# First MLP product of a block in two passes of half its tokens, two chunks of F per PSUM bank

## The chip, the core and the metric

The kernel runs on one core of a Trainium2 chip. Its engines are TensorE (PE in the profile, with PEld for its weight loads), VectorE (DVE), ScalarE (ACT), GpSimd (POOL) and SyncE (SP, which issues DMAs); each works through its own queue in order and waits on semaphores for the others. The metric is the device time of one execution in microseconds; the number compared is the median of several runs.

## What is computed

A block of 2048 tokens of width 640: a layernorm, sliding-window attention of 32 heads of 20 with a window of 256, and beside it an MLP of width 1536 with a squared ReLU, whose output gates the attention's.

```python
xn = _layernorm(x, axis=-1)
s = _A_ref(xn, A_wqkv, A_wo)                     # 32 heads, window 256, output times wo
g = _silu(_B_ref(xn, B_w1, B_b1, B_w2, B_b2))    # relu(xn @ w1 + b1)**2 @ w2 + b2
return x + s * g
```

Every large matrix is carried as a high and a low part in float32r, and a product is made of three: high by high, high by low, low by high.

## The kernel before

**Stages.** A first stage normalizes and transposes the tokens and makes v and the first part of q and k. Then the attention runs in 268 steps of one pair of heads and one tile of 128 tokens each: scores (L493), their transposed form (L542), exponentials on ACT (L549), masks on POOL, splits into float16 parts on ACT and DVE, and the product with v (ops, L481). Last comes the product with wo (L654).

**The filler.** Between the parts of each attention step the function `fill` takes work from one generator, `filler`: the rest of q and k (qkps), then the MLP, in eight blocks. A block is one half of F (768 = 6 chunks of 128, NFH = 6) and one quarter of the tokens (BT = 512). It has a first product (hps: w1 by xn, then bias, ReLU and square) and a second (yps: the squares by w2). Each `yield` names what the piece costs in the plan; `fill` takes pieces until the step's share is reached, and a `yield None` ends the step's filling early.

**Two halves of the array.** The filler's matmuls contract over 128 rows as two matmuls of 64 rows, one on the upper half of TensorE's rows (front, index 0) and one on the lower (back, index 1), which run beside each other. Both add into the same PSUM bank, and a back may not start while the group's fronts still write there. So the fronts of one group are emitted among the backs of the group before. `halves` emits a front through `ahead` and puts the back into the group's `Job`; `ahead` emits backs as long as the plan's clock of the lower half lies behind that of the upper; `open_for` lets a job's backs go only once its `after` is set, which happens with its last front. When its last back is out, `done` queues the evacuation, which `soon` and `flush` emit a little later.

**Banks.** All filler groups share three PSUM banks (`Acc`, tags mm0 to mm2). A group can be opened when one of them has been given back in the program's order (`free`, in the evacuation); if none has, the waiting evacuations are emitted at once. On the chip the group's first matmul then waits until the last reader of that bank is done.

**First product, before.** For each of the six chunks of F one group fills a bank with 128 features of all 512 tokens: 15 matmuls of 512 columns per half. Its evacuation works on two halves of the tokens (MT = 256 columns): ReLU and square on ACT (L951, L952), the exact square on DVE (sq, L954), the low part on POOL (hl, L955). The first half is emitted with `evac`, the second (`rest`, through `late`) a little later, and frees the bank. `hs` holds the chunks whose first half is made, `whole` those that are complete.

**Second product, before.** For each of the block's four tiles of 128 tokens (tt) and each half of the 640 outputs (nh) one group sums 18 matmuls of 320 columns per half over the six chunks; DVE adds the bias or the other half of F's part (ysb, L984) and frees the bank. `product` waits in the program's order until its chunk is in `hs` (tt < 2) or `whole`. For tt = 0 the two groups (nh = 0 and 1) are opened one after the other with the first four chunks each, and then both are ended with the last two (L1008 to L1015).

Of the kernel before, what the change touches and what calls it, by code (L numbers as in the profile page):

```python
# [9 lines left out]
F32 = mybir.dt.float32  # L10
F32R = mybir.dt.float32r
BF16 = mybir.dt.bfloat16
F16 = mybir.dt.float16
AF = mybir.ActivationFunctionType
ALU = mybir.AluOpType

P = 128
S = 2048
D = 640
# [4 lines left out]
KC = D // P  # L24
NP = H // 2
NB = 4
BT = S // NB
# [4 lines left out]
HALF = D // 2  # L32
NFH = F // 2 // P
FHALF = F // 2
MT = 256
# [8 lines left out]
COST = {61: 0.0285, P: 0.067, 2 * P: 0.12, HALF: 0.147, 3 * P: 0.172, BT: 0.23}  # L44
# [9 lines left out]
def f32(ap):  # L54
    return ap.bitcast(F32)
# [3 lines left out]
def attn_mlp_kernel(ctx: ExitStack, tc, x, wqkv, wo, w1, b1, w2, b2, out):  # L59
    nc = tc.nc  # L60
# [47 lines left out]
    b1t = const.tile([P, F // P], F32, name="b1t")  # L108
# [8 lines left out]
    wgt = ctx.enter_context(tc.tile_pool(name="wgt", bufs=2))  # L117
# [19 lines left out]
    with tc.tile_pool(name="ph1v", bufs=2) as p1v, tc.tile_pool(name="ph1", bufs=2) as p1, tc.tile_pool(name="ph1x", bufs=4) as p1b, tc.tile_pool(name="ph1w", bufs=1) as p1w:  # L137
# [137 lines left out]
        with tc.manual_schedule(engines={E_.PE, E_.Activation, E_.DVE, E_.Pool, E_.SP}):  # L275
# [90 lines left out]
            for w in "kq":  # L366
                ps = pat.tile([P, BT // 2], F32, tag="s", name="qkps")
# [111 lines left out]
    def half(j, out, a, b_, **kw):  # L479
        r = slice(j * HP, (j + 1) * HP)  # L480
        return nc.tensor.matmul(out, a[r], b_[r], skip_group_check=True, **kw)  # L481
# [188 lines left out]
        def free(self):  # L670
            banks.append(self.bank)

    def halves(job, ps, a, b_, first, last):
        cost = COST[ps.n]

        def front():
            job.mark = half(0, ps.tile, a, b_, start=first, stop=False)

        def back():
            if first:  # L680
                wait_for(job.mark)
            half(1, ps.tile, a, b_, start=False, stop=last)
        ahead(front, cost)
        job.items.append((back, cost))
        if last:
            job.after = clock[0]

    def open_job(evac, *then):
        def done():
            pending.append(evac)  # L690
            ended.append((mark(), clock[1]))
            for f in then:
                f()
        job = Job(done)
        backlog.append(job)
        return job

    def mm_halves(ps, mms, work, evac, *then):
        job = open_job(evac, *then)
        for j, (a, b_) in enumerate(mms):  # L700
            halves(job, ps, a, b_, j == 0, j == len(mms) - 1)
            yield work
# [9 lines left out]
    def lin1(tiles, off, n):  # L712
        t, o = divmod(off, KC * BT)
        return tiles[t][:, o:o + n]
# [157 lines left out]
    def filler():  # L872
# [5 lines left out]
        for g, b in order_qk:  # L878
# [9 lines left out]
            for w in "qk":  # L888
# [3 lines left out]
                def evac(ps=ps, w=w, g=g, b=b):  # L892
                    vload[0] += 0.7
                    hi = stg.tile([P, BT], F32R, tag="stg", name="shm")
                    lo = stg.tile([P, BT], F32R, tag="stg", name="slo")
                    split(hi, lo, ps.tile)
                    ps.free()
                    posts.extend(qk_stores(w, slice(g * P, (g + 1) * P), slice(b * BT, (b + 1) * BT), hi, lo))
# [19 lines left out]
        for n, (hf, b) in enumerate(blocks):  # L918
            if n % NB == 0:
                ensure(f"1{hf}")  # L920
            if n == NB - 1:
                w1t[1] = queue_w1(1)
                w2t[1] = queue_w2(1)
                shut.update(("11", "21"))
            if n == last:
                wo_part = queue_wo()
                shut.add("o")
            ensure_bulk(its)
            wt1 = w1t[hf]()
            hs, whole, nxt = {}, set(), []  # L930

            def used(n=n, b=b, nxt=nxt):
                if n == NB - 1:
                    shut.discard("11")
                if n == last:
                    shut.discard("o")
                if n < last and blocks[n + 1][1] != b:
                    nxt.extend(load_xb(blocks[n + 1][1]))
            for fc in range(NFH):
                ps = Acc(BT, "hps")  # L940

                def evac(ps=ps, fc=fc, fi=hf * NFH + fc, hs=hs, whole=whole):
                    hh = [stg.tile([P, BT], F32R, tag="stg", name="hh"),
                          stg.tile([P, BT], F32R, tag="stg", name="hl") if fc < NFH - 4 else wgt.tile([P, D], F32R, tag=f"wg{'kq'[fc % 2]}l", name="hl")[:, :BT]]
                    hs[fc] = hh

                    def part(h):
                        vload[0] += 0.5
                        sl = slice(h * MT, (h + 1) * MT)
                        r = at2.tile([P, MT], F32, tag="relu", name="relu")  # L950
                        nc.scalar.activation(r, ps.tile[:, sl], AF.Relu, bias=b1t[:, fi:fi + 1])  # L951
                        nc.scalar.activation(hh[0][:, sl], r, AF.Square)  # L952
                        sq = at2.tile([P, MT], F32, tag="sq", name="sq")
                        nc.vector.scalar_tensor_tensor(sq, ps.tile[:, sl], b1t[:, fi:fi + 1], r, ALU.add, ALU.mult)  # L954
                        nc.gpsimd.tensor_sub(hh[1][:, sl], sq, f32(hh[0][:, sl]))  # L955
                    part(0)

                    def rest():
                        part(1)
                        whole.add(fc)  # L960
                        ps.free()
                    late.append(rest)
                yield from mm_halves(ps, [(lin1(wt1, (wp * KC + c) * FHALF + fc * P, P), xb[xp][:, c * BT:(c + 1) * BT]) for c in range(KC) for wp, xp in ((0, 0), (0, 1), (1, 0))], 0.213, evac, *([used] if fc == NFH - 1 else []))
            if n % NB == 0:
                ensure(f"2{hf}")
            if n == NB:
                load_yin(0)
                load_yin(1)
            wt2 = w2t[hf]()
            for tt in range(4):  # L970
                t = b * 4 + tt
                place = [None]
                jobs = []

                def start(nh, hf=hf, t=t, place=place, idx=4 * (n - NB) + tt, end=n == NB - 1 and tt == 3, n=n, tt=tt):
                    sl = slice(nh * HALF, (nh + 1) * HALF)
                    ps = Acc(HALF, "yps")

                    def evac():
                        vload[0] += 0.5  # L980
                        if not nh:
                            place[0] = wgt.tile([P, D], F32, tag="wgqh", name="ysb")
                        ysb = place[0]
                        nc.vector.tensor_add(ysb[:, sl], ps.tile, (yins[t] if hf else b2t)[:, sl])  # L984
                        ps.free()
                        if nh:
                            post(y_d[hf][:, t, :], ysb)
                            if hf:
                                del yins[t]
                                load_yin(idx + 2)  # L990
                            if end:
                                shut.discard("21")
                    return [ps, open_job(evac), 0]

                def product(jb, nh, fc):
                    ps, job, _ = jb
                    while fc not in (hs if tt < 2 else whole):
                        if pending or late:
                            flush()
                            yield None  # L1000
                        else:
                            drain(backlog, 1)
                    for hp, wp in ((0, 0), (0, 1), (1, 0)):
                        jb[2] += 1
                        halves(job, ps, hs[fc][hp][:, tt * P:(tt + 1) * P], lin1(wt2, (wp * NFH + fc) * D + nh * HALF, HALF), jb[2] == 1, jb[2] == 3 * NFH)
                        yield 0.133
                jbs = {}
                if tt == 0:  # L1008
                    for nh in range(2):
                        jbs[nh] = start(nh)  # L1010
                        for fc in range(NFH - 2):
                            yield from product(jbs[nh], nh, fc)
                    for nh in range(2):
                        for fc in range(NFH - 2, NFH):
                            yield from product(jbs[nh], nh, fc)  # L1015
                else:
                    for nh in range(2):
                        jbs[nh] = start(nh)
                        for fc in range(NFH):
                            yield from product(jbs[nh], nh, fc)  # L1020
                if n == last and tt % 2:
                    load(0)
                    load(1)
            if n < last and nxt:
                xb, its = nxt
            else:
                its = []
# [214 lines left out]
```

## Time and profile before

| | us |
|---|---|
| median of three runs | 1058.17 |
| lowest and highest | 1046.88, 1058.91 |
| the profiled execution | 1057.88 |
| its span, first to last instruction | 1056.2 |

In the profile a line "engine line waited for" tells which instruction an engine stood still before, and which instruction's end released it. The filler's matmuls all stand at L481, so they are told apart by the tile that they write: qkps, hps, yps, and ops for the attention's own. The granted clock is the share of TensorE's clock pulses that its throttle let through. The busy time of PE counts an instruction until its end, so matmuls that run one behind the other overlap in it.

### The profile page before, as it was taken

To read this page: it belongs to the slowest core of one execution; us is meant where nothing else is said; L and a number is where in the kernel's file an instruction comes from. 1 tells how busy PE (TensorE), PEld (TensorE's weight loads), DVE (VectorE), ACT (ScalarE), POOL (GpSimd) and SP (SyncE) were. 2 spreads that over 40 slices of the span, in tenths; PEclk is the share of its full clock that TensorE was granted. 3 is DMA by queue.
4 is the path that set the end of the run, shared out by engine and by line. 5 is a ranking of instruction groups with operands and counts; after the bars stand their busy time and mean duration, and the time that the engine had idled before them with its cause. 6 is when DMAs were issued, how large, how long until landed. Compare 5 with 4: busy or idle time off the path is not lost. (4 is left out here: it accounts for less than half of the span.)

```text
span 1056.2 us, 32767 instructions
## 1 busy us (share of the span) xinstructions
PE 940.2 (89%) x12928; PEld 863.9 (82%) x12928; DVE 754.8 (71%) x2085; ACT 652.1 (62%) x1240; POOL 501.9 (48%) x800
## 2 busy tenths in 40 slices
PE   9999999999998798896897779789889788989998
PEld 9999989988877787786786677678778677878998
DVE  7763689989997686686687678678668756834554
ACT  5533377877887586576477558657747755863221
POOL 5100035755577475566366546557646645652000
PEclk9999999999999998998899899899799889989999
DMA  7996777877853334331542233544254253107674
GB/s 255 344 389 231 218 255 230 252 252 216 257 158 129 107 91 145 90 90 46 170 135 51 83 105 96 155 130 115 65 167 125 56 179 96 34 22 241 247 259 145
DMA packets 106097, 169.77 MB, mean 161 GB/s; under 512 B 42072, under 2 KB 59608, under 8 KB 103384
## 3 DMA queue, kind: packets, MB, share of 16 engines
q1 hardware_dynamic: 105944, 167.68, 50.3%
q8 instruction: 102, 1.67, 0.7%
q14 instruction: 51, 0.42, 0.1%
HBM read 96.15 MB, written 70.91 MB: 158 GB/s over the span
## 5 line engine op out<-in xcount | busy, mean ns | idle before, releaser
L549 ACT ACTIVATE p<-stps,ebias 128x384 f32<-128x384 f32 (+2 forms) x512 | 258.7, 558 | 220.1 <-PE stps L542 126.2
L481 PE MATMUL yps<-w,hh 64*128 64x320 f32 x1536 | 292.0, 340 | 76.1 <-DVE ysb L984 37.5
L503 DVE CUSTOM_DVE_ANT_0 junk<-sps,mask 128x384 bf16<-128x384 f32 (+2 forms) x512 | 250.8, 526 | 129.1 <-PE sps L493 88.6
L550 POOL TENSOR_SCALAR_AFFINE_SELECT p<-p 128x256 f32<-128x256 f32 x256 | 157.8, 616 | 323.1 <-ACT p L549 227.9
L481 PEld LDWEIGHTS yps<-w,hh 64*128 64x128 f32 x1536 | 220.4, 201 | 92.7 <-DVE ysb L984 47.0
L481 PE MATMUL hps<-xb,w 64*128 64x512 f32 x1260 | 256.8, 418 | 21.3 <-DVE ysb L984 10.7
L563 DVE TENSOR_TENSOR pl<-p,ph 128x768 f16<-128x768 f32 (+2 forms) x256 | 243.4, 951 | 16.0 <-PE ops L481 14.0
L481 PE MATMUL ops<-vp,ph 64*128 64x61 bf16 x2880 | 215.1, 193 | 0.1
L481 PE MATMUL yps<-w,hl 64*128 64x320 f32 x768 | 208.1, 333 | 5.8 <-POOL hl L955 5.8
L481 PE MATMUL ops<-vp,pl 64*128 64x61 bf16 x2880 | 212.2, 192 | 0.0
L557 ACT ACTIVATE ph<-p 128x768 f16<-128x768 f32 (+2 forms) x256 | 205.6, 803 | 3.6 <-POOL p L552 2.1
L481 PEld LDWEIGHTS hps<-xb,w 64*128 64x128 f32 x1260 | 175.5, 194 | 34.9 <-DVE ysb L984 13.9
L481 PEld LDWEIGHTS <-ph 64*128 64x128 f16 x2880 | 183.9, 97 | 11.5 <-issue 3.8
L481 PEld LDWEIGHTS <-pl 64*128 64x128 f16 x2880 | 186.9, 97 | 0.3 <-issue 0.3
L481 PEld LDWEIGHTS yps<-w,hl 64*128 64x128 f32 x768 | 135.2, 201 | 7.8 <-POOL hl L955 7.8
L552 POOL TENSOR_SCALAR_AFFINE_SELECT p<-p 128x256 f32<-128x256 f32 x224 | 129.8, 580 | 0.0
L493 PE MATMUL sps<-ks,qs 60*128 60x384 f32 (+2 forms) x512 | 124.2, 370 | 5.4 <-DVE mrow L526 2.2
L542 PE MATMUL stps<-qs,ks 62*128 62x384 f32 (+2 forms) x512 | 112.7, 350 | 0.3 <-DMA qs<-mrow 0.2
L955 POOL TENSOR_TENSOR hl<-sq,hh 128x256 fp32r<-128x256 f32 x96 | 86.0, 900 | 40.8 <-DVE sq L954 31.3
L481 PE MATMUL qkps<-xT,wgkh 64*128 64x512 f32 x320 | 104.0, 400 | 0.0
L481 PE MATMUL qkps<-xT,wgqh 64*128 64x512 f32 x320 | 103.1, 399 | 0.0
L493 PEld LDWEIGHTS sps<-ks,qs 60*128 60x128 f32 x512 | 72.9, 194 | 19.2 <-DVE mt L503 11.7
(110 smaller groups left out, 1613.6 us busy)
## 6 DMA issues: line engine op xcount, KB each, us to landing
ks<-k_d SPq DMA_DIRECT2D x64, 240.0 KB
qs<-q_d SPq DMA_DIRECT2D x64, 240.0 KB
xb<-xs SPq DMA_DIRECT2D x12, 1280.0 KB
xs<-xT SPq DMA_DIRECT2D x8, 1280.0 KB
y<-ysb SPq DMA_DIRECT2D x32, 320.0 KB
k_d<-shm SPq DMA_DIRECT2D x19, 512.0 KB
q_d<-shm SPq DMA_DIRECT2D x19, 512.0 KB
v_d<-vt SPq DMA_DIRECT2D x8, 976.0 KB
```

Of the source, the lines that this page charges most:

```text
L481: return nc.tensor.matmul(out, a[r], b_[r], skip_group_check=True, **kw)
L493: nc.tensor.matmul(r[hh][:, :nk], qs[i][o, q * P:(q + 1) * P], ks[i][o, k0 * P:k0 * P + nk], start=True, stop=True)
L503: nc.vector.tensor_tensor_reduce(out=junk[:, :nk], in0=r[hh][:, :nk], in1=mask[:, 3 * P - nk:], scale=1.0, scalar=-3.0e38, op0=ALU.add, op ...
L542: nc.tensor.matmul(r[hh][:, :n], ks[i][o, kb * P:(kb + 1) * P], qs[i][o, kb * P:kb * P + n], start=True, stop=True)
L549: nc.scalar.activation(p32[:, hh, :n], r[hh][:, :n], AF.Exp, scale=SCALE, bias=ebias)
L550: nc.gpsimd.affine_select(p32[:, :, 0:P], p32[:, :, 0:P], pattern=[[0, 2], [1, P]], compare_op=ALU.is_ge, fill=0.0, base=0, channel_multip ...
L552: nc.gpsimd.affine_select(p32[:, :, 2 * P:], p32[:, :, 2 * P:], pattern=[[0, 2], [-1, P]], compare_op=ALU.is_gt, fill=0.0, base=0, channel ...
L557: nc.scalar.activation(ph[:, :, :n], p32[:, :, :n], AF.Copy)
L563: nc.vector.tensor_sub(pl[:, :, :n], p32[:, :, :n], ph[:, :, :n])
L955: nc.gpsimd.tensor_sub(hh[1][:, sl], sq, f32(hh[0][:, sl]))
```

## The change

A group of the first product now fills its bank with two chunks of F for half of the block's tokens: columns 0 to 255 hold chunk 2 fp, columns 256 to 511 chunk 2 fp + 1, both for the 256 tokens of pass th. There are 30 matmuls of 256 columns per half in place of 15 of 512. Three groups (fp) make the first pass, three more the second; the second product of all four tiles comes behind both. The evacuation keeps its shapes: what was a half of the tokens is now a chunk. `halves` takes an offset and a width in the bank. The second product reads the tile of its half of the tokens and its pair of chunks, waits for complete groups only, and opens its two groups at tt = 0 one after the other like those of the other tiles.

```diff
-    def halves(job, ps, a, b_, first, last):
-        cost = COST[ps.n]
+    def halves(job, ps, a, b_, first, last, o=0, n=None):
+        n = n or ps.n
+        cost, out = COST[n], ps.tile[:, o:o + n]
...
-            for fc in range(NFH):
-                ps = Acc(BT, "hps")
-
-                def evac(ps=ps, fc=fc, fi=hf * NFH + fc, hs=hs, whole=whole):
...
-                yield from mm_halves(ps, [(lin1(wt1, (wp * KC + c) * FHALF + fc * P, P), xb[xp][:, c * BT:(c + 1) * BT]) for c in range(KC) for wp, xp in ((0, 0), (0, 1), (1, 0))], 0.213, evac, *([used] if fc == NFH - 1 else []))
+            for th in range(2):
+                for fp in range(NFH // 2):
+                    ps = Acc(BT, "hps")
+
+                    def evac(ps=ps, th=th, fp=fp, fi=hf * NFH + 2 * fp, hs=hs, whole=whole):
+                        hh = [stg.tile([P, BT], F32R, tag="stg", name="hh"),
+                              stg.tile([P, BT], F32R, tag="stg", name="hl") if fp == 0 else wgt.tile([P, D], F32R, tag=f"wg{'kq'[fp % 2]}l", name="hl")[:, :BT]]
+                        hs[th, fp] = hh
+
+                        def part(i):
+                            vload[0] += 0.5
+                            sl = slice(i * MT, (i + 1) * MT)
+                            r = at2.tile([P, MT], F32, tag="relu", name="relu")
+                            nc.scalar.activation(r, ps.tile[:, sl], AF.Relu, bias=b1t[:, fi + i:fi + i + 1])
+                            nc.scalar.activation(hh[0][:, sl], r, AF.Square)
+                            sq = at2.tile([P, MT], F32, tag="sq", name="sq")
+                            nc.vector.scalar_tensor_tensor(sq, ps.tile[:, sl], b1t[:, fi + i:fi + i + 1], r, ALU.add, ALU.mult)
+                            nc.gpsimd.tensor_sub(hh[1][:, sl], sq, f32(hh[0][:, sl]))
+                        part(0)
+
+                        def rest():
+                            part(1)
+                            whole.add((th, fp))
+                            ps.free()
+                        late.append(rest)
+                    job = open_job(evac, *([used] if (th, fp) == (1, NFH // 2 - 1) else []))
+                    mms = [(i, lin1(wt1, (wp * KC + c) * FHALF + (2 * fp + i) * P, P), xb[xp][:, c * BT + th * MT:c * BT + (th + 1) * MT]) for i in range(2) for c in range(KC) for wp, xp in ((0, 0), (0, 1), (1, 0))]
+                    for m, (i, w_, x_) in enumerate(mms):
+                        halves(job, ps, w_, x_, m == 0, m == len(mms) - 1, i * MT, MT)
+                        yield 0.1065
...
-                    while fc not in (hs if tt < 2 else whole):
+                    while (tt // 2, fc // 2) not in whole:
...
-                        halves(job, ps, hs[fc][hp][:, tt * P:(tt + 1) * P], lin1(wt2, (wp * NFH + fc) * D + nh * HALF, HALF), jb[2] == 1, jb[2] == 3 * NFH)
+                        halves(job, ps, hs[tt // 2, fc // 2][hp][:, fc % 2 * MT + tt % 2 * P:fc % 2 * MT + (tt % 2 + 1) * P], lin1(wt2, (wp * NFH + fc) * D + nh * HALF, HALF), jb[2] == 1, jb[2] == 3 * NFH)
                         yield 0.133
-                jbs = {}
-                if tt == 0:
-                    for nh in range(2):
-                        jbs[nh] = start(nh)
-                        for fc in range(NFH - 2):
-                            yield from product(jbs[nh], nh, fc)
-                    for nh in range(2):
-                        for fc in range(NFH - 2, NFH):
-                            yield from product(jbs[nh], nh, fc)
-                else:
-                    for nh in range(2):
-                        jbs[nh] = start(nh)
-                        for fc in range(NFH):
-                            yield from product(jbs[nh], nh, fc)
+                for nh in range(2):
+                    job = start(nh)
+                    for fc in range(NFH):
+                        yield from product(job, nh, fc)
```

More of the change, by code (lines that the diff above doesn't have):

```diff
@@ L671, in free @@
             banks.append(self.bank)
-    def halves(job, ps, a, b_, first, last):
-        cost = COST[ps.n]
+    def halves(job, ps, a, b_, first, last, o=0, n=None):
+        n = n or ps.n
+        cost, out = COST[n], ps.tile[:, o:o + n]
         def front():
-            job.mark = half(0, ps.tile, a, b_, start=first, stop=False)
+            job.mark = half(0, out, a, b_, start=first, stop=False)
         def back():
@@ L681, in back @@
                 wait_for(job.mark)
-            half(1, ps.tile, a, b_, start=False, stop=last)
+            half(1, out, a, b_, start=False, stop=last)
         ahead(front, cost)
@@ L938, in used @@
                     nxt.extend(load_xb(blocks[n + 1][1]))
-            for fc in range(NFH):
-                ps = Acc(BT, "hps")
-                def evac(ps=ps, fc=fc, fi=hf * NFH + fc, hs=hs, whole=whole):
[L943 to L962, printed above, removed]
-                yield from mm_halves(ps, [(lin1(wt1, (wp * KC + c) * FHALF + fc * P, P), xb[xp][:, c * BT:(c + 1) * BT]) for c in range(KC) for wp, xp in ((0, 0), (0, 1), (1, 0))], 0.213, evac, *([used] if fc == NFH - 1 else []))
```

## The prediction

> **What bounds the kernel now.** I read the page first: the busy shares, then the granted clock.
>
> ```profile
> span 1056.2 us, 32767 instructions
> ...
> PE   940.2 (89%) x12928; PEld 863.9 (82%) x12928; DVE 754.8 (71%) x2085; ACT 652.1 (62%) x1240; POOL 501.9 (48%) x800
> ...
> PEclk9999999999999998998899899899799889989999
> ```
>
> The program took 1057.88 us in this execution, 1.7 us more than its span, and that is the median of the three runs shown (1058.17) to 0.03%. TensorE is busiest, but 116 us of the span it is idle, and from the middle on its clock is not whole. The view of cores gives the clock's mean:
>
> ```profile
> core 0: 1056.2 us, clock 0.955
> ```
>
> 0.045 of 1056 us is 47.5 us of clock not granted. The chain of waits is of no use here: it only reaches back to 974 us, into the last product with wo, which the change leaves alone. So I cut the middle at the places where the first product (hps) and the second (yps) take turns, in the view of stretches (columns: stretch, length, busy time and count of PE, PEld, DVE, ACT, POOL, granted clock, DMA share, GB/s):
>
> ```profile
> 287.00:323.00 36.00, 33.87 (x500) 28.71 (x496) 33.70 (x93) 32.16 (x64) 26.77 (x39) 1.00 0.54 159
> 715.00:748.50 33.50, 31.45 (x533) 28.74 (x533) 28.65 (x86) 27.55 (x56) 23.73 (x38) 1.00 0.45 118
> 748.50:799.50 51.00, 41.82 (x647) 38.01 (x647) 31.24 (x92) 27.00 (x51) 25.24 (x41) 0.83 0.38 118
> ```
>
> The first row is the first product of the first block, the other two are the first and second product of the sixth. Both products are planned as the same amount of filler per attention step, yet the second takes 51 us against 33.5, with DVE at 61% and the clock at 0.83. Nothing is saturated there; TensorE stands still and then runs slowly. Who it waits for in the whole span, and in that last stretch alone (us in total, times, longest):
>
> ```profile
> PE yps L481 <- DVE ysb L984: 37.5, 33, 2.0
> PE yps L481 <- DVE sq L954: 31.5, 14, 4.7
> PE hps L481 <- DVE ysb L984: 10.7, 11, 2.1
> PE hps L481 <- DVE sq L954: 10.2, 12, 2.2
> PE yps L481 <- POOL hl L955: 5.8, 8, 1.0
> PE yps L481 <- ACT hh L952: 5.7, 7, 1.0
> ```
> ```profile
> PE yps L481 <- DVE ysb L984: 5.3, 4, 1.6
> PE yps L481 <- DVE sq L954: 3.4, 2, 1.9
> PE yps L481 <- POOL hl L955: 1.0, 1, 1.0
> ```
>
> These six rows are 101.4 us. sq and ysb do not make data that the waiting matmul reads: they are the last readers of a PSUM bank, so those 89.9 us are waits for one of the three banks. hl and hh (11.5 us) are data: the last chunks of the first product, not yet squared when the second needs them.
>
> **Why the banks come late.** A group of matmuls is emitted in two halves of the rows, the second half (back) one group behind the first (front), and a back can't be emitted before its group's last front has been (Job.after, L447 and L686). At tt = 0 the kernel opens two second-product groups and goes 12 fronts into each before it ends the first (L1008 to L1015). The first group's backs stay locked for those 30 fronts, and once the backs of the last first-product group are out, the lower half of the array has nothing to do. Both halves then run at one rate, so the lag is kept for the groups that follow. I counted in the order in which the programs hand matmuls to TensorE: from the last back of a group to the first matmul that writes its bank again, the median is 68 matmuls where a first-product group follows another, 39 where a second-product group follows a first-product one, 12 between second-product groups, 31 back again. In the changed program these are 110, 78, 52 and 72. The row of 287 to 323 us speaks for this reading: it lies ahead of the first such pair of groups, and there TensorE is busy 33.87 of 36 us at full clock with DVE at 94%.
>
> **The change, part by part.** First, the price. 720 matmuls of 512 columns per half become 1440 of 256, each with its weight load. Rows for both widths, full array, from the timeline (start, length, count):
>
> ```profile
> 15.13 0.76 PE L209 MATMUL qkps<-xT,wgkh 128*128 128x256 f32 x5
> ...
> 18.14 0.76 PE L209 MATMUL qkps<-xT,wgqh 128*128 128x256 f32 x5
> ...
> 38.53 1.33 PE L209 MATMUL qkps<-xT,wgkh 128*128 128x512 f32 x5
> ...
> 43.12 1.29 PE L209 MATMUL qkps<-xT,wgql 128*128 128x512 f32 x5
> ```
>
> 25 of 256 columns from 15.13 to 18.14 are 120.4 ns each; 20 of 512 from 38.53 to 43.12 are 229.5. Per half: 1440 x 0.1204 = 173.4 us against 720 x 0.2295 = 165.2, +8 us. That a pair of halves keeps the full array's pitch is shown at 320 columns:
>
> ```profile
> 604.24 0.36 PE L481 MATMUL yps<-w,hl 64*128 64x320 f32 x2
> 604.39 0.51 PE L481 MATMUL yps<-w,hh 64*128 64x320 f32 x4
> 604.68 0.36 PE L481 MATMUL yps<-w,hl 64*128 64x320 f32 x2
> ```
> ```profile
> 978.68 1.09 PE otp L1083 x10
> 979.77 8.80 PE wops L654 x60
> ```
>
> Six in 0.44 us are 147 ns a pair, and 60 full-array ones in 8.80 us are 147 ns each. At 256 columns no pairs run in this trace. Lower bound: 120.4, the full-array pitch (a gain is excluded, the columns are the same and the loads double). Upper bound: 147, the nearest row of pairs, +38 us more. I take 120.4, because pair and full array agree where both exist. Here the Trainium skill speaks against the change ("TensorE: Matmul & The Clock Gate", Part 3, what overlaps and what doesn't): a weight load overlaps a running matmul only in another row group. By that rule each of the 720 added loads per half would lie bare. By its figure for a load (columns over 1.2, 107 ns) that is 77 us and a time of 1067. The full-array rows disagree: there the load goes to the same rows, 256 further columns cost 229.5 - 120.4 = 109.1 ns, and a load with its matmul of 256 only 11.3 ns more than that. What it would cost is a rival below.
>
> Second, the bank waits. The evacuation time is wait plus distance. Weighted with the pitches above (147 for yps, 229.5 and 120.4 for hps, attention's by their columns, a pair counting one), the median distances are 0.9 us between second-product groups and 1.6 from a first-product group to a second; after the change 2.1 and 3.2. Mean wait on ysb is 37.5/33 = 1.1, so ysb takes about 2.0 us to come; on sq 31.5/14 = 2.25, so about 3.9. Both are far above the operations themselves, it is time in the queue:
>
> ```profile
> L954 DVE SCALAR_TENSOR_TENSOR sq<-hps,b1t,relu 128x256 f32<-128x256 f32 x96 | 46.1, 480 | 38.7 <-ACT relu L951 37.4 <-POOL p L552 0.7 <-POOL on L606 0.4
> L984 DVE TENSOR_TENSOR ysb<-yps,b2t 128x320 f32<-128x320 f32 x32 | 15.2, 474 | 0.0
> ```
>
> After: between second-product groups 2.0 against 2.1 leaves only the spread, which I put at 0.4 us for each of 40 groups, 16 us. Behind a block's last first-product groups the three distances are about 4.5, 3.0 and 1.9 us, so the second group waits 0.9 and the third 2.0, 23 us over eight blocks. The two kinds of hps waits go (3.2 and 4.6 us of distance). Data: tokens of tt = 0 and 1 read only the first pass, three groups old, so hl and hh go. Left 39 of 101.4: -62 us.
>
> Third, the clock. TensorE was busy 41.82 of 51 us where the clock was low, so 0.82 x 47.5 = 39 us of the ungranted clock cost work. Scaled with the waits, 15 are left: -24 us. The trace against a rule: in 748.5 to 799.5 the clock fell to 0.83 with no wait over 1.9 us. The Trainium skill ("TensorE: Matmul & The Clock Gate", Part 1, The HAM clock gate) has the clock halved after an idle window of about 3.4 us; by it waits of 2 us would never gate, and all 39 us would come back, 975 in all. The row disagrees, so I keep 15.
>
> Fourth, what comes late next. In second-product stretches DVE goes from 31.24 of 51 to 31.24 of some 40 us (an eighth of the 86 us gone), 78%, near the share of first-product stretches (28.65 of 33.5, 86%), where waits on sq came to 10.2 us in eight blocks. I add +10 for that.
>
> At nothing: the evacuations keep their shapes and number (96 sq, 96 hl), half of a bank is now a chunk of F in place of half the tokens; tile counts per pool are unchanged; the next block's loads are still queued by the last group's end (used), ahead of the same SP entries, and DMA is at a share of 0.38. The filler's price per group is the same 3.2 us, so the pacing stays.
>
> Sum: 1057.9 + 8 - 62 - 24 + 10 = 990 us.
>
> **Rivals.** (a) All waits go: 1058 + 8 - 101 - 39 = 926. For it: the stretch of 287 us. Against it: the 1.9 us of distance behind each first product.
> (b) The bank waits stay, because sq and ysb sit in DVE's queue and that only moves with it. Then only the data waits go, 11.5 us and their 4 us of clock: 1058 + 8 - 16 = 1050. For it: DVE releases 89.9 of the 101.4. Against it: the first row of stretches, DVE 94% busy and no stall.
> (c) Bare loads within a half. 128-column matmuls with a load each run at 109 ns (otp, 10 in 1.09), so a load costs no more; 720 of them are 78 us: 990 + 78 = 1068.
> (d) Slower: the two halves' loads share one path. Then a pair costs two loads, 2 x 109 = 218 ns, in place of 120.4; 1440 x 0.098 = 141 us in the first-product stretches: 1131. It beats the gains from 167 ns a pair on ((1058 - 990)/1440 = 47 ns above 120.4). At 512 columns such loads hide, which would be why nothing shows now. Against it: 147 ns a pair at 320 columns, with two loads in it, and the loads' own row, where 1260 x 194 ns = 244 us lie in 175.5 us of time, so they do overlap.
>
> ```profile
> L481 PEld LDWEIGHTS hps<-xb,w 64*128 64x128 f32 x1260 | 175.5, 194 | 34.9 <-DVE ysb L984 13.9 <-issue 10.4 <-PE hps L481 5.1
> ```
>
> **How the numbers follow.** Forecast 0.60, alone 955 to 1028 (the 38 us of the pair's upper bound one way; half of the 39 us of left waits and the clock the other). (a) 0.10, (b) 0.14, (c) 0.04, (d) 0.12. A measurement of this kernel tells about 2%, 21 us, from no change: the forecast and (a) are faster, 0.70; (b) and (c) within, 0.18; (d) slower, 0.12. The range 940 to 1055 takes in the forecast, half of (a) and (b), 0.79.
>
> **What would show it.** Right: PE's waits on sq under 25 us and on ysb under 20, none on hl and hh; mean clock 0.98; second-product stretches of 40 to 42 us; hps pairs of 256 columns every 120 ns; first-product stretches no longer than 36. Wrong: pairs at 150 ns or more (c, d); waits on ysb and sq still near 90 us (b); or the same waits gone from TensorE, but its steps as long as before with DVE or ACT full, which would make the time 1040 or more with no term of mine to blame but the fourth.

## The result, and the profile after

The changed kernel takes 955.41 us (median of three runs, 954.27 to 956.62) against 1058.17: a ratio of 0.906 with a 95% interval of 0.897 to 0.915. The profiled execution is the one of 955.41 us, its span 953.7. The forecast was 990, with a range of 940 to 1055.

The page of the changed kernel, busy shares and granted clock, and the view of cores:

```profile
PE 898.4 (94%) x14368; PEld 850.3 (89%) x14368; DVE 757.3 (79%) x2085; ACT 648.0 (68%) x1240; POOL 507.4 (53%) x800
...
PEclk9999999999999999999999999999999999999999
```
```profile
core 0: 953.7 us, clock 0.991
```

DVE, ACT and POOL do the work that they did, and TensorE has 1440 matmuls more, yet is busy 42 us less. TensorE's waits in the changed kernel (us in total, times, longest; sq is now L956, ysb L990):

```profile
PE yps L481 <- DVE sq L956: 24.1, 15, 2.6
PE yps L481 <- DVE ysb L990: 10.6, 15, 2.2
...
PE hps L481 <- DVE ysb L990: 2.5, 5, 0.9
```

37.2 us are left of 101.4; hh and hl are in no row. Where the time came from is read from stretches cut at every change between first and second product. The last row of such an answer sums its stretches; here are the eight first-product and then the eight second-product stretches before the change:

```profile
sum 288.90, PE 264.71 PEld 237.24 DVE 242.07 ACT 230.21 POOL 196.61; mean PE 33.09 PEld 29.66 DVE 30.26 ACT 28.78 POOL 24.58
```
```profile
sum 395.90, PE 314.01 PEld 285.81 DVE 245.16 ACT 223.29 POOL 198.37; mean PE 39.25 PEld 35.73 DVE 30.65 ACT 27.91 POOL 24.80
```

and the same two after it, the second with the row of the sixth block, whose stretch the prediction showed at 51 us and a clock of 0.83:

```profile
sum 274.10, PE 267.88 PEld 255.64 DVE 245.19 ACT 231.34 POOL 202.74; mean PE 33.49 PEld 31.95 DVE 30.65 ACT 28.92 POOL 25.34
```
```profile
685.70:722.50 36.80, 31.98 (x620) 30.11 (x614) 31.24 (x93) 27.14 (x51) 25.38 (x39) 1.00 0.52 159
...
sum 304.50, PE 266.29 PEld 251.70 DVE 244.25 ACT 217.62 POOL 196.55; mean PE 33.29 PEld 31.46 DVE 30.53 ACT 27.20 POOL 24.57
```

91 of the 102 us come from the second product, 15 from the first, and the rest of the kernel is 4 us longer. The second product now takes 38 us a block, where it took 49; the first takes 34. In the row shown the clock is whole, in the other seven it is between 0.92 and 1.00.

### The profile page after: what moved, and what is told of

It reads as the page before. It is cut to its first block, busy times and chain, and to the rows that moved or that the text cites. A ratio compares the mean times of both kernels' runs of the same rounds, so it can differ in the third digit from the quotient of the medians.

```text
span 953.7 us, 35554 instructions
## 1 busy us (share of the span) xinstructions
PE 898.4 (94%) x14368; PEld 850.3 (89%) x14368; DVE 757.3 (79%) x2085; ACT 648.0 (68%) x1240; POOL 507.4 (53%) x800
## 4 chain that ended last, share of the span: by engine, by line
PE 59%; DVE 20%; ACT 12%; issue 6%; POOL 3%; DMA 0%; DVEq 0%; ACTq 0%; POOLq 0%
PE yps L481 14%; PE ops L481 8%; PE wops L654 7%; PE vps L232 7%; PE qkps L481 6%; DVE junk L503 6%; DVE pl L563 5%; ACT p L549 5%; PE hps L481 5%; PE sps L493 4%; DVE sq L956 3%; PE qkps L209 3%; PE stps L542 3%; ACT relu L953 2%; ACT ph L557 2%
## 5 line engine op out<-in xcount | busy, mean ns | idle before, releaser
L481 PE MATMUL yps<-w,hh 64*128 64x320 f32 x1536 | 256.9, 320 | 35.1 <-DVE sq L956 24.1
L481 PE MATMUL hps<-xb,w 64*128 64x256 f32 x2520 | 236.5, 285 | 2.5 <-DVE ysb L990 2.5
L481 PEld LDWEIGHTS yps<-w,hh 64*128 64x128 f32 x1536 | 197.8, 190 | 43.9 <-DVE sq L956 27.8
L481 PEld LDWEIGHTS hps<-xb,w 64*128 64x128 f32 x2520 | 221.1, 187 | 4.1 <-DVE ysb L990 4.1
L481 PE MATMUL ops<-vp,ph 64*128 64x61 bf16 x2880 | 203.8, 190 | 0.1
L481 PE MATMUL ops<-vp,pl 64*128 64x61 bf16 x2880 | 201.7, 189 | 0.0
L481 PE MATMUL yps<-w,hl 64*128 64x320 f32 x768 | 193.4, 320 | 0.0
L481 PEld LDWEIGHTS <-pl 64*128 64x128 f16 x2880 | 177.1, 94 | 0.1
L481 PEld LDWEIGHTS <-ph 64*128 64x128 f16 x2880 | 174.4, 94 | 2.2 <-PE stps L542 0.6
L481 PEld LDWEIGHTS yps<-w,hl 64*128 64x128 f32 x768 | 122.9, 189 | 0.0
```

## The experiments

Two theories stood against each other. L: the interleaved pair of groups at tt = 0 locks the backs, the lower half of the array falls behind and stays behind, and every bank comes late. D: what costs is the late last chunk, and the pair only hides it.

**One part alone: no pair.** The kernel before, with the second product's plain order for all tiles:

```diff
-                jbs = {}
-                if tt == 0:
...
-                else:
-                    for nh in range(2):
...
+                for nh in range(2):
+                    job = start(nh)
+                    for fc in range(NFH):
+                        yield from product(job, nh, fc)
```

> The kernel before, with one edit: at tt = 0 the second product's two groups run one after the other, as for the other tiles; the first product keeps its 512 columns and whole tokens. Theory L (the interleaved pair locks the backs and makes every bank late): in the order of instructions the distance between second-product groups grows from a mean of 1.0 to 2.2 us, so TensorE's waits on ysb fall from 48 to about 15 us and the 10 us of first-product groups on sq go; at each block's start the last chunk isn't made when nh = 0 asks for it, so waits on hh and hl of some 5 us a block, 40 in all, take the place of 43; mean clock 0.97; about 995 us. Theory D (the late chunks are what costs, the pair hides them): the data waits grow and nothing else changes, 1055 to 1075 us.

965.03 us, ratio 0.914 (0.908 to 0.920). Its waits:

```profile
PE yps L481 <- ACT hh L952: 10.1, 13, 1.9
PE yps L481 <- POOL hl L955: 8.8, 13, 1.1
PE yps L481 <- DVE ysb L984: 6.6, 11, 0.9
...
PE hps L481 <- DVE sq L954: 2.2, 6, 0.6
```

D is out: this one edit, which makes the data later, brings nine tenths of the whole gain. The waits on banks fall from 89.9 to 9.0 us (with 0.2 of hps on ysb). I expected 995. Of the 30 us between, 21 are the data waits, on which I put 40 and which are 18.9, and 8 are the waits on ysb, 6.8 in place of 15.

**The other part alone: the pair put back.** The changed kernel with the lines that the first diff takes out, on its own two passes:

> The changed kernel, with one edit: at tt = 0 the interleaved pair of groups of the kernel before is put back; the two passes stay. Theory L: the distances fall to those of the kernel before (mean 1.1 us between second-product groups, 2.2 behind the first product), so waits on ysb come back to some 45 us and on sq to some 35, none on hh and hl, mean clock 0.965, about 1020 us. Theory D: the chunks are early all the same, so at most 965 us.

1023.14 us, ratio 0.970 (0.965 to 0.974); expected 1020. The two passes without the change of order are worth 32 us. The data waits are gone and the clock is 0.973, but the banks are late as before:

```profile
PE yps L481 <- DVE sq L956: 44.0, 20, 4.5
PE yps L481 <- DVE ysb L990: 33.7, 31, 2.0
PE hps L481 <- DVE ysb L990: 9.7, 10, 2.0
PE hps L481 <- DVE sq L956: 5.3, 6, 1.4
```

**The pair once.** The pair in the first of eight blocks only:

```diff
-                if tt == 0:
+                if tt == 0 and n == 0:
```

> The changed kernel, with the interleaved pair put back in the first of the eight blocks alone. Theory L says that the lag of the lower half, once made, is kept, since both halves then run at one rate and nothing in the two-pass order empties the queue of backs: in the order of instructions the distance between second-product groups is 1.1 us in all blocks, as with the pair in every block. So waits on ysb of 40 to 48 us spread over all blocks, sq some 30, about 1010 to 1020 us. If the lag ends with its block: waits on ysb some 15 us, 955 to 963 us.

1009.43 us, ratio 0.960 (0.950 to 0.970). The first block's second product is over at 365 us. The waits from 420 us on, which is the end of the second block and all later ones, none of which has a pair:

```profile
PE yps L481 <- DVE sq L956: 30.8, 16, 3.7
PE yps L481 <- DVE ysb L990: 29.1, 27, 2.1
PE hps L481 <- DVE ysb L990: 7.9, 8, 2.0
PE hps L481 <- DVE sq L956: 5.2, 6, 1.4
```

The pair in one block alone costs 54 us, where the pair in every block costs 68 (against the changed kernel). In the order of instructions the distance between second-product groups is 1.1 us in all blocks, as with the pair in every block, against 2.0 in the changed kernel. That is the lag being kept, seen by itself.

**The lag made by hand.** The changed kernel with the pause before a filler group's backs longer by 1.8 us of plan, no matmul added:

```diff
-        return queue and queue[0].after is not None and max(clock[1:]) >= queue[0].after + SETTLE
+        return queue and queue[0].after is not None and max(clock[1:]) >= queue[0].after + (SETTLE + 1.8 if queue is backlog else SETTLE)
```

> The changed kernel, with the backs of each filler group held 1.8 us longer in the plan before they may be emitted; no matmul is added or taken away. Theory L (a lag of the lower half is kept and shortens every bank's distance): mean distance between second-product groups 0.2 us in place of 2.0, waits on ysb 80 to 120 us, on sq about 60, mean clock about 0.92, 1060 to 1100 us. If the distance isn't what matters: 955 to 965 us.

1084.2 us, ratio 1.027 (1.022 to 1.033): slower than the kernel before. Its waits, and its clock:

```profile
PE yps L481 <- DVE sq L956: 49.9, 23, 4.6
PE yps L481 <- DVE ysb L990: 48.7, 39, 3.1
PE hps L481 <- DVE sq L956: 19.8, 24, 1.8
PE qkps L481 <- DVE slo L113: 16.3, 18, 1.8
PE hps L481 <- DVE ysb L990: 12.9, 13, 1.7
```
```profile
core 0: 1082.1 us, clock 0.973
```

The time is as expected, and the waits on sq (69.7 in all) are near the 60 that I put. The wait on ysb (61.6 in all) is under the 80 to 120 expected, and the clock is 0.973 where I had 0.92. The edit holds back the groups of q and k too: the waits on slo are theirs, so not all of the loss lies in the MLP.

**The price of narrow matmuls, with late banks.** The kernel before, each first-product matmul of 512 columns cut into two of 256:

```diff
-                yield from mm_halves(ps, [(lin1(wt1, ...), xb[xp][:, c * BT:(c + 1) * BT]) ...], 0.213, evac, ...)
+                mms = [(o, lin1(wt1, ...), xb[xp][:, c * BT + o:c * BT + o + MT]) ... for o in (0, MT)]
+                for m, (o, w_, x_) in enumerate(mms):
+                    halves(job, ps, w_, x_, m == 0, m == len(mms) - 1, o, MT)
+                    yield 0.1065
```

> The kernel before, with each first-product matmul of 512 columns cut into two of 256 with the same weights (1440 more matmuls and weight loads, order of groups, banks and evacuations unchanged, the interleaved pair kept). Price by the full array's pitches: +8 us, 1066 (1060 to 1072), pairs every 121 ns. If the halves' loads share one path: pairs every 147 to 218 ns, 1095 to 1200 us. If the finer pieces themselves bring the gain (backs fit better beside fronts): under 1045 us.

1039.23 us, ratio 0.986 (0.980 to 0.993): 16 us faster, where I expected 8 slower. The waits on ysb stay, those on sq fall from 41.7 to 30.7, and the clock rises to 0.970:

```profile
PE yps L481 <- DVE ysb L989: 37.0, 32, 2.0
PE yps L481 <- DVE sq L955: 25.3, 13, 3.8
PE hps L481 <- DVE ysb L989: 10.6, 11, 2.1
...
PE hps L481 <- DVE sq L955: 5.4, 9, 1.4
```

In the order of instructions the distance between first-product groups is 3.7 us here and 3.3 before, which fits the fall of the hps waits on sq from 10.2 to 5.4. The distances to and between second-product groups are as before, so neither the fall of the yps waits on sq nor the better clock is explained.

**The same price, with banks in time.** The same cut without the pair:

> The kernel before without the interleaved pair (965 us) and with its first-product matmuls cut from 512 to 256 columns. Where the pair was kept the cut took 16 us off, where the pitches say +8. If that gain was only backs coming a little earlier in a kernel whose banks were late, then here, where banks are early, the price shows: first-product stretches 267 + 7 = 274 us in sum, 970 to 974 us in all. If narrower matmuls fit better beside the other half in themselves: 945 to 955 us.

974.81 us, ratio 0.926 (0.917 to 0.935): 9.8 us more than with 512 columns and without the pair, though on another chip, on which the kernel before took 1058.4 us and not 1055.6. So narrow matmuls gain nothing here, and that what they brought in the run before was time against late banks is inferred from this. The price isn't where I looked for it: the first-product stretches, which I expected at 274 us in sum against 267.3 with 512 columns, are 269.7.

```profile
sum 269.70, PE 264.35 PEld 252.49 DVE 243.60 ACT 232.48 POOL 205.25; mean PE 33.04 PEld 31.56 DVE 30.45 ACT 29.06 POOL 25.66
```

Most of the added time lies in the second product (335.4 us in sum against 325.2), where the waits on ysb are 12.3 us in place of 6.6.

**More distance behind the first product.** The 24 us on sq stand behind a block's last first-product groups. Two of these moved between second-product groups:

```diff
+            mixed = n % NB != 0
...
                 for nh in range(2):
+                    if mixed and (tt, nh) in ((0, 1), (1, 0)):
+                        yield from first(1, tt + 1)
                     job = start(nh)
```

> The changed kernel, with the last two first-product groups of a block moved between the second product's first groups (blocks 2 to 4 and 6 to 8): the order is hps, yps, hps, yps, hps, yps where it was three hps and then yps. The 24 us of waits on sq stand behind the block's last first-product groups, where the distance falls to 3.0 and 1.9 us; in the mixed order it is 2.5 to 3.7. If those waits are distance: sq some 10 us, about 940 us. If they are DVE's and ACT's queues: they come up before other groups and the time stays at 950 to 960.

962.28 us, ratio 0.913 (0.904 to 0.923), 7 us worse than the changed kernel. The time lies outside both ranges of the expectation. The waits on sq are what they were (24.1), as the second of its theories has it: a longer distance on paper did not shorten them. And the data became late (hl and hh, 10.8 us in all), since the first group of the second product now comes one group after the last chunk that it reads:

```profile
PE yps L481 <- DVE sq L955: 23.4, 19, 2.4
PE yps L481 <- POOL hl L956: 8.5, 10, 1.6
PE yps L481 <- DVE ysb L996: 6.3, 9, 1.7
```

**Evacuation sooner.** The second half of the evacuation emitted at once behind the first, for the last two first-product groups:

```diff
-                        late.append(rest)
+                        if th and fp:
+                            rest()
+                        else:
+                            late.append(rest)
```

> The changed kernel, with the second half of the evacuation emitted at once behind the first (not 0.6 us of plan later) for the last two first-product groups of a block. Same waits on sq: distance theory, 24 to about 18 us and 948 to 952 us; if the queues of ACT and DVE set the end of the evacuation, 953 to 960.

951.63 us, ratio 0.904 (0.893 to 0.916). To tell 4 us from two chips' difference, it ran again beside the changed kernel, with two edits on top of it that lengthen the distances: SETTLE from 0.45 to 0.2, and LEAD from 0.15 to 0.4 (each alone).

> The changed kernel once more, on the chip and beside the runs of the three that follow, so that differences of under one per cent between them can be told: 953 to 957 us.

> The changed kernel with the second half of the evacuation emitted at once for the last two first-product groups of a block, once more: 4 us below the changed kernel if what was seen (951.6 against 955.4) holds on one chip; within 2 us of it if that was the difference of two chips.

> The version before this one, with the plan's pause between a group's last front and its first back cut from 0.45 to 0.2 us (filler and attention): every distance grows by 0.2 us on average. By distance alone 3 to 6 us faster, some 947 us. Rival: the back then stands in TensorE's queue before the group's fronts have left the array and holds up everything behind it, some hundred groups and 128 attention products by up to 0.25 us each, 950 to 975 us.

> The version of the second run of this call, with the lower half allowed 0.4 us ahead of the upper in the plan, not 0.15: distances grow by 0.4 us between second-product groups, with the pause of 0.45 us kept. By distance alone waits on ysb from 14 to some 6 us and on sq from 18 to some 12, about 942 us. Rival: backs emitted ahead of their pairing fronts leave the upper half alone for a while, 950 to 960 us.

| version | median us, lowest to highest | ratio to before, interval |
|---|---|---|
| the changed kernel | 955.45, 954.94 to 958.93 | 0.907, 0.903 to 0.911 |
| evacuation at once | 952.11, 951.29 to 953.01 | 0.903, 0.899 to 0.907 |
| and SETTLE 0.2 | 947.96, 947.35 to 949.4 | 0.900, 0.896 to 0.903 |
| and LEAD 0.4 | 947.20, 942.08 to 950.48 | 0.898, 0.894 to 0.902 |

The runs of the first three versions do not overlap: 3 us for the evacuation, 4 more for the pause; neither rival showed. With LEAD 0.4 the waits are

```profile
PE yps L481 <- DVE sq L956: 12.0, 12, 2.1
PE yps L481 <- DVE ysb L993: 9.2, 13, 1.9
```

against 18.1 and 10.8 with the evacuation alone: the sq waits did as expected, the ysb waits hardly moved, and 947 is 5 us above what I put. With SETTLE 0.2 they are 15.4 and 8.5. These two versions beat both kernels; the two edits were not tried together.

## Why the prediction held, step by step

**The bound.** "TensorE stands still and then runs slowly": shown. Most signs named beforehand came: sq waits under 25 us, ysb under 20, pairs near 120 ns. The second-product stretches and the clock came out better than named (38 us and 0.991 for 40 to 42 and 0.98), and two first-product stretches are over the 36 us named (36.7 and 36.4). Of the 102 us, 91 came out of the second-product stretches, with the work of DVE, ACT and POOL unchanged.

**Why the banks come late.** The reading of the pair was a reading of code and order; the four runs on it (no pair, pair back, pair once, lag by hand) show it in both directions, and the rival (b), that sq and ysb wait in DVE's queue whatever the order, is refuted by the first of them. The mixed order shows its limit: there the distances on paper were better and the waits on sq were not.

**The bank waits and data waits, -62 us.** Measured: 101.4 to 37.2, -64. By kinds: sq 24.1 against 23 forecast, ysb 13.1 against 16, hh and hl none. Wait plus distance as the time that an evacuation takes was a good rule for this change; for the mixed order and for the ysb waits with LEAD 0.4 it was not.

**The price, +8 us.** Pairs of 256 columns run in the changed kernel as its timeline shows (start, length, count; the length holds the last one's own 0.28 us):

```profile
660.71 1.56 PE L481 MATMUL hps<-xb,w 64*128 64x256 f32 x22
```

(1.56 - 0.28)/21 = 61 ns, 122 a pair; forecast were 120.4. Bare loads (c) and a shared path (d) are out. What the term comes to in the whole kernel is less sure: +9.8 us without the pair (974.81 against 965.03), of which the first-product stretches show only 2.4, and in the changed kernel first-product stretches of 274.1 us against these without the pair at 512 columns:

```profile
sum 267.30, PE 260.88 PEld 234.88 DVE 242.17 ACT 231.89 POOL 202.74; mean PE 32.61 PEld 29.36 DVE 30.27 ACT 28.99 POOL 25.34
```

**The clock, -24 us.** Not granted were 47.5 us before and are 0.009 x 954 = 8.6 now; by the same 0.82 that is 32 us of work, 8 more than the term. The scaling with the waits is wrong as a rule: the lag by hand has over 150 us of such waits and a clock of 0.973, as has the version without the pair with 28. It came near here by luck of the case.

**What comes late next, +10 us.** This term has the wrong sign, and most of the 35 us between 990 and 955 lies here. With waits -64, clock -32 and price +8, the rest is -102 + 88 = -14: DVE at 80% of the second-product stretches (244 of 304.5) stalls TensorE hardly more than the two waits say (the waits of the attention's scores on it grew by 2.5 us), and something was gained beyond waits and clock. An estimate from the programs' order and the traces, with each matmul of a half counted at its pitch: between the first hps and the last yps only one half of the array is at work for some 125 us before and 68 after, for 110 without the pair and for 80 with the pair put back. The size depends on the way of counting (two others, at a shorter pitch and for the filler's matmuls alone, give a fall of 30 us), but in each the fall goes with the two passes more than with the order of the pair. As two halves side by side need half the time of one behind the other, it is worth 15 to 28 us and would cover the 14; no run isolates it.

**Why two passes at all.** Without the pair the last chunk is asked for before it is made; the program then emits that group's backs in one go, and the lower half runs alone. In that version's timeline:

```profile
544.47 0.41 PE L481 MATMUL yps<-w,hl 64*128 64x320 f32 x1 [0.27 <-POOL hl L955]
544.47 1.65 PE L481 MATMUL hps<-xb,w 64*128 64x512 f32 x6
```

Two passes take that away, 965 to 955 us, in spite of the price. The waits alone don't tell this gain: they are 27.9 us without the pair and 37.2 in the changed kernel. What got better is the clock, 0.973 to 0.991, and by the estimate above the time with one half alone; how the 10 us divide between them isn't shown.

## What to carry to other kernels

Where work is emitted in order for two units that run at one rate, an order that blocks one of them even once can be paid in every later group, as here: look for the lag that is kept, and count the distance from a buffer's last writer to its next use in the order of instructions, group by group. A wait for a buffer plus that distance is an estimate of the time that its release takes; here it priced the waits of this change to 2 us before it ran, but not those of the mixed order. An interleaving that hides one late datum is worth a run without it.

## What the runs showed of the hardware

Loads of 128 columns for both halves fit beside matmuls of only 256: pairs every 122 ns, against 120.4 for one full-array matmul of that width. And the clock does not follow the sum of the waits: with no wait over 1.9 us it was granted at 0.83 for 51 us in the kernel before, while the changed kernel's row of 685.7 to 722.5 us has waits up to 2.0 us at 1.00, and 150 us of waits, up to 4.6 long, left 0.973 over the whole run with the lag made by hand. What decides it stays open.
